# A third block of tokens on its own condition, and a small second block whose low parts lie beside its high parts

## The chip, the cores and the metric

The kernel runs on one core of one Trainium2 chip. The metric is the device time of one execution in microseconds (us); the median of several runs is compared with that of the changed kernel.

## The reference

Chunked attention feeds a dense layer pair with a gated activation, and that feeds a mixture of eight experts. Only the expert part is touched:

```python
expert_idx = np.argmax(x @ w_gate, axis=1)      # one expert for each of 1536 tokens
for i in range(N):                              # the first `capacity` = 384 tokens of each expert
    ...
h = np.maximum(np.einsum('ecd,edf->ecf', disp, w1), 0.0)   # 512 -> 1024
y = np.einsum('ecf,efd->ecd', h, w2)                       # 1024 -> 512
out[i] = gate_w[i] * y[expert_idx[i], pos[i]]
```

Worked out from the reference with its inputs, the experts get, in the order in which the kernel takes them (`EORDER`), 224, 291, 128, 160, 128, 256, 160 and 189 tokens. They are called e0 to e7 here, by place in that order.

## The kernel before, in words

Every product of two 32-bit numbers is made of three TensorE matmuls: each operand is held as a rounded high part and a low part (the remainder), and high x high, high x low and low x high are added up in PSUM. An expert's tokens come in blocks of 128, gathered by GpSimd (`load`, L808), transposed by TensorE (`trans`, L825) and split by ScalarE and VectorE (L829, L830).

The code for one expert from e1 on is two arms of a branch on the token count, read from a register by each engine (L1260). Up to 128 tokens, the arm `one` runs the first block alone (`block`: 64 matmuls with its transposes). Above, the arm `more` runs two blocks together: `layer1` (96 matmuls of 256 columns, L858; its high parts by ScalarE, L861, its low parts by VectorE, L862), the transposes of the next expert's two blocks (`next_trans`), `layer2` of block 0 (24 matmuls of 512 columns, L925: 8 pieces of 128 rows, three products each), and then `rest`. In `rest` a second branch (L963) asks for more than 256 tokens: if so, it transposes block 2, runs `layer2` of block 1 and the whole `block` 2; if not, only `layer2` of block 1. Whichever block comes last leaves its result in the PSUM tile `ylast`, and `after_arms` scales it (ScalarE, L945) and sends it to its rows of `out` (GpSimd, L946). The other blocks are scaled and sent where they end. The order of the sends is fixed: each writes `out`, so each waits until the one before has landed.

e0 has a code of its own (`after_first`), with the branches L992 and L1000, whose bodies are skipped with these inputs. In a `with tc.If` without an else, an engine that skips the body first waits until its own earlier work is done.

Inside each arm ScalarE and VectorE also split the weights for this expert's second layer and the next expert's first one (L289 and L294, eight pieces of 128x1024 each in `more`). A scheduler decides the order of the instructions on each engine within a stretch without branches, by the order of the code and priorities; the branch itself is one such piece, which it may put ahead of work written earlier.

```python
hi, lo = t[:, 0, :, o:o + P], t[:, 1, :, o:o + P]   # a split tile: [part, piece, token]
for n, (hz, wz) in enumerate(((0, 0), (0, 1), (1, 0))):
    nc.tensor.matmul(ps, lhsT=h[:, hz, fc, o:o + P], rhs=w[:, wz, fc % 4, :], ...)
```

Of the kernel before, what the change touches and what calls it, by code (L numbers as in the profile page):

```python
# [9 lines left out]
F32 = mybir.dt.float32  # L10
# [6 lines left out]
ALU = mybir.AluOpType  # L17
# [4 lines left out]
P = 128  # L22
# [65 lines left out]
def kernel(  # L88
# [14 lines left out]
    nc = tc.nc  # L103
# [19 lines left out]
    F2 = F // P  # L123
    NCB = max(2, -(-cap // P))
# [128 lines left out]
    class Piece(SimpleNamespace):  # L253
# [19 lines left out]
        def rest(self, act=True):  # L273

            low = self.words()[0].bitcast(U32)
            self.r = w_pools["work"].tile([P, KC, P], I32, tag="rest", name="rest")
            if act:
                nc.scalar.activation(out=self.r, in_=low, func=AF.Copy, scale=2.0 ** -29)
            else:
                nc.vector.tensor_scalar(out=self.r, in0=low, scalar1=2.0 ** -29, scalar2=None, op0=ALU.mult)  # L280
# [90 lines left out]
    def w_tile(name, i):  # L371
        while (name, i) not in ready:
            assert flight or wide or w_can_load(), name
            w_pump()
        return where[name].rearrange("p z (c f) -> p z c f", f=512)
# [424 lines left out]
    def expert_parts(e, ep, tp, cnt):  # L800

        ex = EORDER[e]
# [19 lines left out]
        def trans(b):  # L822
            ps = psum("t", "pst")
            for c in range(KC):
                nc.tensor.transpose(ps[:, c * P:(c + 1) * P], xr[b][:, c * P:(c + 1) * P], ident)  # L825
            t, o = xs_of(b)
            hi, lo = t[:, 0, :, o:o + P], t[:, 1, :, o:o + P]
            pv = ps.rearrange("p (c n) -> p c n", n=P)
            act = nc.scalar.activation(out=hi, in_=pv, func=AF.Copy)  # L829
            dve = nc.vector.tensor_tensor(out=lo, in0=pv, in1=hi.bitcast(F32), op=ALU.subtract)  # L830
            return act.ins, dve.ins

        def gate(b):
            sm = tp.tile([P, 1], F32, tag="gs", name="gs")
            nc.scalar.activation(out=tp.tile([P, E], F32, tag="ex", name="ex"), in_=xr[b][:, DM:DM + E], func=AF.Exp, accum_out=sm)  # L835
            g = tp.tile([P, 1], F32, tag="gt", name="gt", bufs=8)
            nc.vector.tensor_scalar(out=sm, in0=sm, scalar1=EPS, scalar2=None, op0=ALU.add)
            nc.vector.reciprocal(out=g, in_=sm)
            gt[b] = g
# [88 lines left out]
        def layer2(b, last):  # L928
            ps = y_of(last)
            layer2_part(b, ps, range(F2))  # L930
            evacuate(b, ps, last)

        ylast = []

        def evacuate(b, ps, last):
# [19 lines left out]
        def after_arms():  # L955
            send(*ylast)

        def rest(b):

            if b == NCB:  # L960
                layer2(b - 1, True)
                return
            with tc.If(cnt[ex] > b * P) as more:  # L963
                trans(b)
                layer2(b - 1, False)
                gate(b)
                later(b)
            with more.Else():
                layer2(b - 1, True)

        def later(b):
            block(b, True)

        def next_trans():
            if e + 1 < E:
# [30 lines left out]
        def more():  # L1006

            for b in range(2, NCB):
                load(b)
            for fc in range(F2):  # L1010
                mm, act = layer1(fc)
                if fc == GFC:
                    after_act = act
                if fc == TFC:
                    after_mm = mm
                if fc in PUMPS:
                    w_next(e)
            with tc.issue_after(after_act):
                for b in range(2):
                    gate(b)  # L1020
            with tc.issue_after(after_mm):
                next_trans()
            layer2(0, False)
            with tc.high_priority(offset=-LOWER2):
                while w_next(e):
                    pass
            rest(2)
        return SimpleNamespace(load=load, trans=trans, xs_of=xs_of, one=one, more=more, after_first=after_first,
                               before_arms=before_arms, after_arms=after_arms)


    with ExitStack() as st:
# [34 lines left out]
        def after_attention(_):  # L1067
# [21 lines left out]
            n=lambda g: step_n(g, nc.vector), N=lambda g: step_n(g, nc.gpsimd), d=step_d, p=step_p, e=step_e,  # L1089
# [130 lines left out]
    with ExitStack() as st:  # L1220
        wp3 = ctx.enter_context(tc.tile_pool(name="wp3", bufs=1, side="left"))
        ep = st.enter_context(tc.tile_pool(name="ep", bufs=1, side="right"))
        tp = st.enter_context(tc.tile_pool(name="tp", bufs=2, side="right"))
        pst = st.enter_context(tc.tile_pool(name="ps_t", bufs=2, space=PSUM))
        ps2 = st.enter_context(tc.tile_pool(name="ps_h2", bufs=4, space=PSUM))
        ps3 = st.enter_context(tc.tile_pool(name="ps_y", bufs=1, space=PSUM))
        ps_pools["t"] = (pst, "t", [P, 512])
        ps_pools["h"] = (ps2, "h", [P, 512])
        ps_pools["y"] = (ps3, "y", [P, 512])
        ps_pools["yl"] = (ps3, "yl", [P, 512])  # L1230
        free_slots.append(wp3.tile([P, 2, 2048], F32R, name="w5"))
        late_raw(RAWS)
        parts = [expert_parts(e, ep, tp, cnt) for e in range(E)]
        not_before.append(parts[0].load(1))
        with ExitStack() as behind:
            for i in parts[0].trans(1):
                behind.enter_context(tc.issue_after(i))
            w_loads(8)
            while w_next(-1):
                pass  # L1240
        w_end[0] = len(pieces)
        with tc.high_priority(offset=LOADS):
            w_loads(8 * (F // 512))
        not_before.clear()
        for e in range(E):
            if e + 1 < E:
                for b in range(2):
                    parts[e + 1].load(b)
                parts[e + 1].xs_of(0)
            if e == 0:  # L1250
                with tc.high_priority(offset=LOADS):
                    w_loads(8 * (F // 512))
                first_block.send()
                parts[0].after_first()
            else:
                parts[e].before_arms()
                with tc.high_priority(offset=LOADS):
                    w_loads(8 * (F // 512))
                before = w_state()
                with tc.If(cnt[EORDER[e]] > P) as full:  # L1260
                    parts[e].more()
                after = w_state()
                w_back(before)
                with full.Else():
                    parts[e].one()
                assert w_state() == after
                parts[e].after_arms()
            for j in range(F // 512):
                w_free(("w1", e, j))
            for j in range(F // 512):  # L1270
                w_free(("w2", e, j))
# [70 lines left out]
```

## Time and profile before

| | us |
|---|---|
| median of three runs | 543.0 (542.32 to 543.14) |
| the profiled execution | 540.01 |
| its span, first to last instruction | 538.2 |
| TensorE (PE) busy | 516.9, 96% of the span |
| VectorE (DVE) busy | 311.0, 58% |
| ScalarE (ACT) busy | 272.6, 51% |
| GpSimd (POOL) busy | 85.1, 16% |

The profiled execution took 3.0 us less than the median of the runs. PE is the instruction stream of the matmuls, PEld the loading of their stationary operand, which runs beside them. In a row of the timeline, the bracket says how long the engine sat idle before it and what ended that; "issue" is time in which it waited for nothing that the profile shows, and a trailing q (PEq) is the engine's sequencer. An engine's clock (PEclk) is the granted share of its full speed.

### The profile page before, as it was taken

The page shows a single profiled execution, that of the slowest core. Times are in us where ns is not written, and L with a number is a line of the kernel's source. Part 1 is how long each engine was busy: PE and PEld are TensorE (multiplying, and loading weights), DVE is VectorE, ACT ScalarE, POOL GpSimd, SP SyncE. Part 2 cuts the span into 40 slices and gives each one's busy share as a digit, 9 for nine tenths or more (in the row PEclk, how much of TensorE's full clock was granted, in tenths as well). Part 3 has the DMA queues.
Part 4 walks back from the last instruction along what each step waited for, and adds up shares of the span by engine and source line. Part 5 has one row for each costly group of instructions (what it writes and reads, how often), then busy time and mean ns, then how long its engine had stood idle before and what let it go on. Part 6 is the DMA issues. An engine that isn't in the chain of part 4 may idle for free. (4 is left out here: it accounts for less than half of the span.)

```text
span 538.2 us, 10665 instructions
## 1 busy us (share of the span) xinstructions
PE 516.9 (96%) x4211; PEld 445.0 (83%) x4211; DVE 311.0 (58%) x627; ACT 272.6 (51%) x551; POOL 85.1 (16%) x92
## 2 busy tenths in 40 slices
PE   8898999999999999999999999999988997999995
PEld 4686888899988999889988887779777976989893
DVE  4899799995229722228375446457314944947250
ACT  2786879773237422235254334457235925938231
POOL 3211012222001100004100000232022222201111
PEclk9999999999999999999999999999998998999999
DMA  8985654342003530000168213597524884885000
GB/s 287 328 315 193 238 174 141 120 158 79 1 0 119 184 130 1 1 0 2 37 210 264 80 41 98 161 319 260 181 62 160 269 324 146 279 328 196 23 26 31
DMA packets 38955, 80.29 MB, mean 149 GB/s; under 512 B 4009, under 2 KB 10153, under 8 KB 38890
## 3 DMA queue, kind: packets, MB, share of 16 engines
q1 hardware_dynamic: 36010, 70.66, 38.3%
q0 software_dynamic: 2880, 8.74, 5.1%
q8 instruction: 43, 0.70, 0.5%
q14 instruction: 22, 0.18, 0.1%
HBM read 69.90 MB, written 10.27 MB: 149 GB/s over the span
## 5 line engine op out<-in xcount | busy, mean ns | idle before, releaser
L584 PE MATMUL acc<-w,g 128*128 128x512 f32 x576 | 153.3, 400 | 1.1 <-DVE w L294 0.7
L541 PEld LDWEIGHTS psh<-xT,w 128*128 128x128 f32 x1152 | 146.7, 188 | 7.4
L541 PE MATMUL psh<-xT,w 128*128 128x256 f32 x1152 | 151.1, 280 | 0.0
L584 PEld LDWEIGHTS acc<-w,g 128*128 128x128 f32 x576 | 100.6, 188 | 21.5 <-issue 2.1
L556 ACT ACTIVATE sg<-psh 128x256 f32<-128x256 f32 x96 | 36.8, 384 | 128.2 <-PE psh L541 127.8
L294 DVE TENSOR_TENSOR w<-raw,w 128x1024 fp32r<-128x1024 f32 x64 | 77.2, 1220 | 41.5 <-ACT w L289 38.0
L564 DVE TENSOR_TENSOR g<-sg,g 128x256 fp32r<-128x256 f32 x87 | 40.3, 463 | 77.8 <-ACT g L560 74.7
L925 PE MATMUL psy<-w,hT 128*128 128x512 f32 x336 | 82.7, 400 | 0.3 <-ACT y L945 0.3
L925 PEld LDWEIGHTS psy<-w,hT 128*128 128x128 f32 x336 | 62.0, 188 | 15.3 <-ACT y L945 0.6
L289 ACT ACTIVATE w<-raw 128x1024 fp32r<-128x1024 f32 x64 | 66.3, 1060 | 2.8 <-PE acc L584 2.2
L858 PEld LDWEIGHTS psh<-xs,w 128*128 128x128 f32 x480 | 58.0, 188 | 1.1 <-issue 0.7
L858 PE MATMUL psh<-xs,w 128*128 128x256 f32 x480 | 58.3, 282 | 0.3 <-PEq L1000 0.3
L560 ACT ACTIVATE g<-psh 128x256 fp32r<-128x256 f32 x96 | 36.2, 380 | 0.0
L595 DVE SCALAR_TENSOR_TENSOR x<-acc,x 128x512 f32<-128x512 f32 x36 | 24.3, 687 | 18.2 <-PE acc L584 18.0
L880 PE MATMUL psh<-w,xs 128*128 128x512 f32 x96 | 27.4, 438 | 7.0 <-ACT w L289 2.9
L880 PEld LDWEIGHTS psh<-w,xs 128*128 128x128 f32 x96 | 19.6, 210 | 12.7 <-issue 7.2
L808 POOL DMA_INDIRECT xr<-rows,taker x20 | 24.2, 1211 | 23.6 <-DVE w L294 16.9
L294 DVE TENSOR_TENSOR w<-w,w 128x512 fp32r<-128x512 f32 x27 | 21.6, 802 | 9.5 <-ACT w L289 9.3
L270 DVE SCALAR_TENSOR_TENSOR w<-raw,w 128x512 int32<-128x512 int32 x32 | 23.4, 734 | 0.1
L259 ACT ACTIVATE w<-raw 128x512 f32<-128x512 f32 x32 | 21.1, 670 | 1.4 <-DMA raw<-in_w_out_dram 1.2
L289 ACT ACTIVATE w<-w 128x512 fp32r<-128x512 f32 x32 | 20.0, 628 | 3.5 <-POOL w L284 2.0
L284 POOL TENSOR_TENSOR w<-w,rest 128x512 int32<-128x512 int32 x8 | 12.1, 1507 | 60.8 <-DVE w L270 55.0
(134 smaller groups left out, 487.2 us busy)
## 6 DMA issues: line engine op xcount, KB each, us to landing
raw<-in_w_dram SPq DMA_DIRECT2D x64, 512.0 KB, 5.0
raw<-in_w_in_dram SPq DMA_DIRECT2D x16, 512.0 KB, 3.8
raw<-in_w_out_dram SPq DMA_DIRECT2D x16, 512.0 KB, 3.3
vt<-in_v_dram SPq DMA_DIRECT2D x12, 512.0 KB, 3.6
kt<-in_k_dram SPq DMA_DIRECT2D x12, 368.0 KB, 6.7
qt<-in_q_dram SPq DMA_DIRECT2D x12, 256.0 KB, 4.1
out_dram<-blank SPq DMA_DIRECT2D x12, 256.0 KB, 4.2
rows<-x SPq DMA_DIRECT2D x5, 520.0 KB, 4.1
```

The source lines that it names most:

```text
L289: nc.scalar.activation(out=w_dst(self.name, self.i, 0), in_=w, func=AF.Copy)
L294: eng.tensor_tensor(out=lo, in0=w, in1=hi.bitcast(F32), op=ALU.subtract)
L541: nc.tensor.matmul(ps, lhsT=w[:, wz, c, i * P:(i + 1) * P], rhs=xT[tb][:, xz, c, :], start=n == 0, stop=n == 3 * KC - 1)
L556: nc.scalar.activation(out=sg_t[u], in_=h_t[u], func=AF.Silu, scale=1.702)
L560: g_last[:1] = [nc.scalar.activation(out=g[:, 0], in_=h_t.pop(u), func=AF.Silu, scale=1.702).ins]
L564: lo = eng.tensor_tensor(out=g[:, 1], in0=sg_t.pop(u), in1=g[:, 0].bitcast(F32), op=ALU.subtract)
L584: nc.tensor.matmul(acc_t[tb][s], lhsT=g[:, gz, s * P:(s + 1) * P], rhs=w[:, wz, wi, :], start=i == 0 and n == 0, stop=u == last_of(k, tb) ...
L595: nc.vector.scalar_tensor_tensor(out=dst, in0=acc_t[tb][s], scalar=1 / 1.702, in1=dst, op0=ALU.mult, op1=ALU.add)
L808: return nc.gpsimd.indirect_dma_start(out=t, out_offset=None, in_=rows[:, :], in_offset=bass.IndirectOffsetOnAxis(ap=taker[:, b, ex:ex + 1 ...
L858: mm = nc.tensor.matmul(ps, lhsT=w[:, wz, c, f0:f0 + P], rhs=t[:, xz, c, :], start=m == 0, stop=m == 3 * KC - 1)
L880: nc.tensor.matmul(p1[j], lhsT=x[:, xz, c, o:o + P], rhs=w[:, wz, c, :], start=(xz, wz, c) == (0, 0, 0), stop=(xz, wz, c) == (1, 0, KC - 1))
L925: nc.tensor.matmul(ps, lhsT=h[:, hz, fc, o:o + P], rhs=w[:, wz, fc % 4, :], start=fc == 0 and n == 0, stop=fc == F2 - 1 and n == 2)
```

## The change

Two things. `rest` is taken out of the arm `more` and becomes a condition of its own, behind `after_arms`, for every expert from e1 on (so also behind the arm `one`): above 256 tokens it transposes block 2 and runs it, with its own send. And in `more`, where the second block has at most 64 tokens (an expert of at most 192: here e3, e6 and e7), a new `layer2_few` runs the second layer of that block. VectorE copies the low parts of its 64 tokens into the columns beside the 64 high parts, so that one matmul of the pair multiplies both with the high part of the weights (rows 0 to 63 and 64 to 127 of the result), and a second one of 64 columns adds high x low. At the end VectorE adds the lower half of the result to the upper one. Otherwise `layer2` of block 1 runs as before, into `ylast`.

```diff
+        def layer2_few(b):
+            n = P // 2
+            h = hT_of(b)
+            o = b * P
+            nc.vector.tensor_copy(h[:, 0, :, o + n:o + P], h[:, 1, :, o:o + n])
+            ps = y_of(True)
+            for fc in range(F2):
+                w = w_tile(("w2", e, fc // 4), (fc % 4) // 2)
+                both = [(ps, h[:, 0, fc, o:o + P], w[:, 0, fc % 4, :]), (ps[:n], h[:, 0, fc, o:o + n], w[:, 1, fc % 4, :])]
+                for i, (out_, x, y) in enumerate(both if fc < F2 - 1 else both[::-1]):
+                    nc.tensor.matmul(out_, lhsT=x, rhs=y, start=fc == 0 and i == 0, stop=fc == F2 - 1 and i == 1)
+            t = ep.tile([P, 512], F32, tag="hs", name="few", bufs=2)
+            nc.vector.tensor_copy(t[:n], ps[n:])
+            nc.vector.tensor_tensor(out=ps[:n], in0=ps[:n], in1=t[:n], op=ALU.add)
+            evacuate(b, ps, True)
...
-        def rest(b):
-            if b == NCB:
-                layer2(b - 1, True)
-                return
-            with tc.If(cnt[ex] > b * P) as more:
-                trans(b)
-                layer2(b - 1, False)
-                gate(b)
-                later(b)
-            with more.Else():
-                layer2(b - 1, True)
+        def rest():
+            for b in range(2, NCB):
+                with tc.If(cnt[ex] > b * P):
+                    trans(b)
+                    gate(b)
+                    block(b, False)
...
             layer2(0, False)
             with tc.high_priority(offset=-LOWER2):
                 while w_next(e):
                     pass
-            rest(2)
+            with tc.If(cnt[ex] < P + P // 2 + 1) as small:
+                layer2_few(1)
+            with small.Else():
+                layer2(1, True)
...
                 parts[e].after_arms()
+                parts[e].rest()
```

On TensorE, the arm `more` of e6 stood like this, from the transposes of the next expert's blocks on (psy is the result of a `layer2`, L963 the branch in `rest`):

```order
L825 MATMUL pst<-ident,xr 128x128 x8
L925 MATMUL psy<-w_94,hT 128x512 x12
L925 MATMUL psy<-w_93,hT 128x512 x12
L963 COMPARE_AND_BRANCH
L825 MATMUL pst<-ident,xr 128x128 x4
...
L963 UNCONDITIONAL_BRANCH
L925 MATMUL psy<-w_94,hT 128x512 x12
L925 MATMUL psy<-w_93,hT 128x512 x12
L963 UNCONDITIONAL_BRANCH
```

It now stands like this (L1036 is the branch on 192 tokens, L944 the matmuls of `layer2_few`):

```order
L825 MATMUL pst<-ident,xr 128x128 x8
L925 MATMUL psy<-w_94,hT 128x512 x5
L1036 COMPARE_AND_BRANCH
L944 MATMUL psy<-w_94,hT 128x512
L944 MATMUL psy<-w_94,hT 64x512
...
L1036 UNCONDITIONAL_BRANCH
L925 MATMUL psy<-w_94,hT 128x512 x12
L925 MATMUL psy<-w_93,hT 128x512 x12
L1036 UNCONDITIONAL_BRANCH
L925 MATMUL psy<-w_94,hT 128x512 x7
L925 MATMUL psy<-w_93,hT 128x512 x12
```

The branch with the second block has moved into the second layer of block 0: five of its 24 matmuls stand ahead, 19 behind.

On VectorE, the end of the same arm of e6 was this (L294 splits a weight piece, L862 writes a low part of the first layer, L830 that of the next expert's tokens):

```order
L294 TENSOR_TENSOR w_4506<-raw_3_3362,w_4506 128x1024 [waits DMAHW6_49]
L862 SCALAR_TENSOR_TENSOR hT<-psh,hT 128x256 [waits Activation_49]
L830 TENSOR_TENSOR xs<-pst,xs 128x4x128 [waits Activation_49] x2
L963 COMPARE_AND_BRANCH
```

And now it is this:

```order
L862 SCALAR_TENSOR_TENSOR hT<-psh,hT 128x256 [waits Activation_49]
L830 TENSOR_TENSOR xs<-pst,xs 128x4x128 [waits Activation_49]
L1036 COMPARE_AND_BRANCH
L938 COPY hT<-hT 128x8x64 [waits DVE_49]
L946 COPY few<-psy 64x512 [waits PE_49]
L947 TENSOR_TENSOR psy<-psy,few 64x512 [waits DVE_49]
L1036 UNCONDITIONAL_BRANCH
L1036 UNCONDITIONAL_BRANCH [waits DVE_49]
L830 TENSOR_TENSOR xs<-pst,xs 128x4x128 [waits Activation_49]
```

The copy of the low parts stands behind all the weight pieces, the last low part of the first layer and one of the two L830.

On GpSimd, the end of the program (e7) was this, with the send of block 0 (y, taker) ahead of the branch and that of `ylast` (y, tl) behind the arms:

```order
L946 DMA out_dram<-y,taker 1536x512 [waits DMASW5_49,Activation_49]
L963 COMPARE_AND_BRANCH
...
L946 DMA out_dram<-y,tl 1536x512 [waits DMASW5_49,DMASW7_49,DMASW0_49,Activation_49]
```

And now it is this:

```order
L1036 UNCONDITIONAL_BRANCH
L963 DMA out_dram<-y,taker 1536x512 [waits DMASW5_49,DMASW4_49,Activation_49]
L1272 UNCONDITIONAL_BRANCH
...
L963 DMA out_dram<-y,tl 1536x512 [waits DMASW5_49,DMASW7_49,DMASW4_49,Activation_49]
L978 COMPARE_AND_BRANCH
```

The send of block 0 has moved behind the second block's branch, next to the last send, which waits for it (DMASW7).

## Rows read from the trace of the kernel before

**Rows 1.** The page: its head and part 1 (busy time of each engine).

```profile
span 538.2 us, 10665 instructions
PE 516.9 (96%) x4211; PEld 445.0 (83%) x4211; DVE 311.0 (58%) x627; ACT 272.6 (51%) x551; POOL 85.1 (16%) x92
```

**Rows 2.** Groups of TensorE by line: busy us, mean ns, idle before.

```profile
L925 PE MATMUL psy<-w,hT 128*128 128x512 f32 x336 | 82.7, 400 | 0.3 <-ACT y L945 0.3
L858 PE MATMUL psh<-xs,w 128*128 128x256 f32 x480 | 58.3, 282 | 0.3 <-PEq L1000 0.3
```

**Rows 3.** Timeline of TensorE, e6 and e7: start, length, what.

```profile
496.64 1.03 PE L825 MATMUL pst<-ident,xr 128*128 128x128 f32 x8
497.43 11.48 PE L925 MATMUL psy<-w,hT 128*128 128x512 f32 x48
508.75 11.59 PE L858 MATMUL psh<-xs,w 128*128 128x256 f32 x96
520.18 11.40 PE L925 MATMUL psy<-w,hT 128*128 128x512 f32 x48
```

**Rows 4.** Timeline of TensorE, the third block of e1 and the start of e2.

```profile
383.34 0.60 PE L825 MATMUL pst<-ident,xr 128*128 128x128 f32 x4
384.28 5.88 PE L925 MATMUL psy<-w,hT 128*128 128x512 f32 x24 [0.34 <-ACT y L945]
390.00 4.36 PE L880 MATMUL psh<-w,xs 128*128 128x512 f32 x18
405.14 5.99 PE L880 MATMUL psh<-w,xs 128*128 128x512 f32 x18 [2.91 <-ACT w L289]
```

**Rows 5.** Timeline of TensorE, e3's second layer and the start of e4.

```profile
432.13 11.49 PE L925 MATMUL psy<-w,hT 128*128 128x512 f32 x48
444.63 0.47 PE L880 MATMUL psh<-w,xs 128*128 128x512 f32 x1 [1.01 <-ACT y L945]
447.38 5.47 PE L880 MATMUL psh<-w,xs 128*128 128x512 f32 x17 [2.28 <-issue]
```

**Rows 6.** Windows after those two waits: length, busy times by engine, granted clock, DMA.

```profile
407.00:409.00 2.00, 2.00 (x6) 1.52 (x6) 0.00 (x0) 0.00 (x0) 1.00 (x1) 0.50 0.90 282
447.30:449.00 1.70, 1.62 (x4) 1.28 (x4) 0.00 (x0) 0.00 (x0) 1.39 (x2) 0.50 0.59 178
```

**Rows 7.** Timeline of TensorE behind the skipped branches L992 and L1000 of e0.

```profile
351.63 4.48 PE L880 MATMUL psh<-w,xs 128*128 128x512 f32 x18 [0.83 <-ACT xs L829]
365.32 11.69 PE L858 MATMUL psh<-xs,w 128*128 128x256 f32 x96 [0.32 <-PEq L1000]
```

**Rows 8.** Timeline of VectorE at the end of the first layer: e3, e6, e7.

```profile
434.99 1.28 DVE L830 TENSOR_TENSOR xs<-pst,xs 128x512 fp32r<-128x512 f32 x2
499.34 1.28 DVE L830 TENSOR_TENSOR xs<-pst,xs 128x512 fp32r<-128x512 f32 x2
520.80 0.42 DVE L862 SCALAR_TENSOR_TENSOR hT<-psh,hT 128x256 fp32r<-128x256 f32 x1 [0.99 <-ACT hT L861]
```

**Rows 9.** Groups of VectorE by line and shape: one source, and two.

```profile
L263 DVE TENSOR_SCALAR w<-w 128x512 f32<-128x512 f32 x32 | 14.8, 471 | 7.2 <-ACT w L259 7.2
L830 DVE TENSOR_TENSOR xs<-pst,xs 128x512 fp32r<-128x512 f32 x16 | 10.4, 685 | 5.2 <-ACT xs L829 5.0
```

**Rows 10.** Timeline of ScalarE at e1's third block: send's scaling, gate, token split.

```profile
383.54 0.69 ACT L945 ACTIVATE y<-psy,gt 128x512 f32<-128x512 f32 x1 [4.97 <-PE psy L925]
384.12 0.20 ACT L835 ACTIVATE ex<-xr 128x8 f32<-128x8 f32 x1
384.31 0.59 ACT L829 ACTIVATE xs<-pst 128x512 fp32r<-128x512 f32 x1
```

**Rows 11.** The end: GpSimd's last two sends, and the first one's flight in the chain.

```profile
526.98 1.00 POOL L946 DMA_INDIRECT out_dram<-y,taker  x1 [14.09 <-ACTq L963]
532.71 1.00 POOL L946 DMA_INDIRECT out_dram<-y,tl  x1 [4.42 <-ACT y L945]
526.98 2.76 DMA out_dram<-y,taker
```

More of the change, by code (lines that the diff above doesn't have):

```diff
@@ L956, in after_arms @@
             send(*ylast)
-        def rest(b):
-            if b == NCB:
-                layer2(b - 1, True)
-                return
-            with tc.If(cnt[ex] > b * P) as more:
-                trans(b)
-                layer2(b - 1, False)
-                gate(b)
-                later(b)
-            with more.Else():
-                layer2(b - 1, True)
-        def later(b):
-            block(b, True)
+        def rest():
[4 more added lines that the diff above has]
+                    block(b, False)
         def next_trans():
@@ L1026, in more @@
                     pass
-            rest(2)
-        return SimpleNamespace(load=load, trans=trans, xs_of=xs_of, one=one, more=more, after_first=after_first,
+            with tc.If(cnt[ex] < P + P // 2 + 1) as small:
+                layer2_few(1)
+            with small.Else():
+                layer2(1, True)
+        return SimpleNamespace(load=load, trans=trans, xs_of=xs_of, one=one, more=more, rest=rest, after_first=after_first,
                                before_arms=before_arms, after_arms=after_arms)
```

## The prediction

> **What bounds the kernel now.** I read the page first: TensorE is busy for 516.9 of 538.2 us [rows 1], so time is won or lost where its stream gets shorter or has holes. Then the groups by line, to see which arms ran: 480 matmuls at L858 are five passes through `more` of 96 each [rows 2], as the token counts say (e1, e3, e5, e6, e7); of these e3, e6 and e7 have at most 192 tokens. Then TensorE's timeline through the experts. From e6 to e7 there is no hole at all: 11.48 us of second layers end where the next first layer starts [rows 3]. So a matmul taken out there is worth its full time, and a wait put in costs its full time. The holes stand elsewhere: at e1's third block [rows 4] and where the arm `one` starts, at e2 (2.91 us) and e4 (1.01 and, after a single matmul, 2.28 us, "issue") [rows 4, 5]. Last, VectorE and ScalarE where the first layer ends, since the new copy queues there, and the chain at the end of the program.
>
> All terms go against the profiled execution, 540.0 us; the median of the runs is 543.0, and I add the sum to that.
>
> **The matmuls saved.** `layer2_few` has 16 in place of 24. A matmul of 512 columns comes every 11.40 / 48 = 0.238 us [rows 3], and one of 256 columns every 11.59 / 96 = 0.121 us: the moving columns set the pace, not the width of the result. So the 64-wide ones cost 0.238 us too, and eight less are worth 1.9 us, three times: **-5.7 us**. If the 64-wide ones were quicker, at most some tenths more.
>
> **The copy ahead of them.** The first L944 waits for the copy of the low parts. Before, the second block's matmuls came after 24 others; now only five stand ahead, because the branch has moved into block 0's second layer. Nothing behind a waiting matmul can pass it, so the 19 others, which need nothing new, wait too. When would TensorE be there, and when is the copy done?
> - e3: TensorE at 432.13 + 5 x 0.239 = 433.3 [rows 5]. VectorE is late with its weight pieces: its L830 pair starts at 434.99 and one of the two takes 0.64 [rows 8], so it ends at 435.6. The copy moves 512 numbers per partition from SBUF to SBUF; the trace has none, the nearest is a one-source instruction of that size, 0.47 us, the dearer bound a two-source one that reads PSUM, 0.69 [rows 9]. I take 0.47, and 0.1 each for VectorE's branch and for the wake-up (an estimate; the skipped branch of rows 7 cost TensorE 0.32 for both). Done at 436.3: **3.0 us** of waiting.
> - e6: TensorE at 497.43 + 1.19 = 498.6 [rows 3], the copy done at 499.34 + 0.64 + 0.67 = 500.65 [rows 8]: 2.0 us. Ahead of e6, ScalarE now has the sends of both blocks of e5 to scale, one more at 0.58 us from start to start [rows 10], before it can start on the weights that VectorE waits for; TensorE is itself 0.3 later (below). So 2.3 us.
> - e7: no next expert, so no L830 and few weight pieces. TensorE at 520.18 + 1.19 = 521.4, the last low part done at 520.80 + 0.42 [rows 3, 8], the copy at 521.9: 0.5 us.
>
> Together **+5.8 us** (5.3 to 6.8 with the bounds for the copy and the branch). What follows the matmuls, VectorE's second copy and the addition, some 1.2 us by rows 9, lies beside the 19 matmuls of 4.5 us and costs nothing. So `layer2_few` by itself saves nothing.
>
> **The clock after a hole.** [...] After the hole of 0.83 us the pace was not hurt (18 in 4.48) [rows 7]. The new holes of 3.0 and 2.3 us lie between, close to the larger; I count one fall, **+1.5 us** (0 to 3.0).
>
> **The branch of its own.** Where there are no more than 256 tokens, each engine waits for its own work and jumps over the body. The trace has this: L1000 cost TensorE 0.32 us before e1 [rows 7]. It now stands ahead of e3, e5, e6 and e7 with nothing else to wait for: 4 x 0.32 = **+1.3 us**; ahead of e4 it lies in the hole that is there, behind e7 beside the last sends.
>
> **The third block of e1.** Before, its tokens were transposed ahead of block 1's second layer, and the 24 matmuls covered the split: transposes and wait took 384.28 - 383.34 = 0.94 us [rows 4]. Now nothing covers it. From the last matmul, ScalarE starts after 0.2 us, scales two sends (0.58 each), does the gate (0.19) and splits (0.59) [rows 10], with 0.1 for its branch 2.3 us until the block can start: **+1.4 us**. Bounds: 0.3, if the split came ahead of the sends as in rows 7 (0.83 of waiting plus transposes), and 2.0.
>
> **The end.** Before, e7's block 0 was sent beside the last matmuls. Now its send starts when they end, and the last one waits until it has landed. The first send took 2.76 us from its issue [rows 11], and the second can't start before: **+2.8 us**; the scaling of the second hides in that.
>
> **The start of e2.** There TensorE jumps from the end of e1 over an arm and a whole `more`. Counting matmuls jumped over with nothing executed in between: 324 ahead of e2 (24 + 64 + 236), 300 ahead of e4, both with a hole that the profile puts to nothing but "issue" at TensorE's weight load; 64 ahead of e6 and e7, and there no hole [rows 3 to 5]. Now `more` has 168, and ahead of e2 the body of the third block is executed: 168 are left. That is nearer to 64 than to 300, so I take the hole to shrink to the one that a wait for the send leaves, 1.01 us as at e4: -1.9, and the slow clock behind it goes, -1.63: **-3.5 us** (0 to -4.5). Ahead of e4 there are 292, and I leave it as it is; ahead of e6 and e7 124, and I count nothing.
>
> **Sum:** -5.7 + 5.8 + 1.5 + 1.3 + 1.4 + 2.8 - 3.5 = +3.6 us, 543.6 by the profiled execution, **546.6 us** as a median.
>
> **The rivals.**
> - *The hole at e2 stays.* For it: 168 matmuls are still more than twice what was jumped over freely. Then +3.5: 550.1 us. Chance 0.25. [...]
> - *More holes.* Both new waits bring the clock down, or one of the jumps of 124 matmuls shows: +1.5 to +3.3, around 549.5 us. Chance 0.14.
> - *The hole at e4 closes too*, because the jump over it is now made in three steps, with a stop of the sequencer at the skipped branch: -2.28 - 1.35, 543.0 us, no change. Against it: the distance is the same. Chance 0.11.
> - *The copy is in time* (the other side). If VectorE were through with its pieces when TensorE gets there, 5.8 and 1.5 us go: 539.3 us, faster. It decides where the two waits of e3 and e6 together stay under 1.5 us and the clock holds. For it: the lag is not VectorE's nature, at e7, with half the weight pieces, it is nearly gone [rows 8]; a slower TensorE elsewhere could let it catch up. Against it: at e3 and e6 the copy stands behind all eight pieces on VectorE, and the changes at the borders delay ScalarE, which feeds them. Chance 0.08.
>
> **Numbers.** The forecast has a chance of 0.42 (545 to 548.3 on its own). The range from 543.0 to 551.0 us leaves out the fourth rival and the upper tail. A measurement of this kernel can tell about 0.2%, 1.1 us, from no change: faster 0.09, same 0.12, slower 0.79.
>
> **What would show it.** In the changed kernel's timeline: 16 L944 in about 3.8 us, three times; TensorE's wait ahead of the first, put to VectorE's L938, near 3.0, 2.3 and 0.5 us; granted clock 0.5 behind one of them; 0.3 us ahead of e3, e5, e6 and e7, put to PEq; some 2.3 us from e1's second layers to its third block, ended by ScalarE's L829; e2's first matmul about 1 us after e1's last, without a slow stretch; and the last send issued some 3.9 us after the last matmul (1.1 before), behind the landing of the other. The forecast is wrong if L944 starts without a wait, if e2 keeps its hole, or if the holes bring the clock down more often than once.

## The result and the profile after

The changed kernel takes 549.2 us (median of 6 runs, 547.0 to 550.1), the kernel before beside it 542.7 us: a ratio of 1.0125, with a 95% interval from 1.009 to 1.016. That is +6.5 us, where +3.6 had been forecast; 549.2 lies inside the range of 543 to 551. The profiled execution took 550.0 us with a span of 548.2. Some 3.2 us of the 10.0 us between the two spans lie ahead of the changed code (the transposes ahead of e0's last block stand at 353.37 in place of 350.21), where runs of one kernel differ, too (353.37 and 350.63 in two executions of the change); behind that point the change costs 6.8 us, which fits the medians. Two executions in the sets of the experiments below took 1014 and 1020 us, nearly twice as long as all the others, and are left out of every median and ratio.

First the page's head and its part 1, against [rows 1]:

```profile
span 548.2 us, 10729 instructions
PE 514.4 (94%) x4183; PEld 440.9 (80%) x4187; DVE 319.0 (58%) x636; ACT 273.8 (50%) x551; POOL 87.4 (16%) x92
```

Then groups of TensorE by line, against [rows 2]:

```profile
L925 PE MATMUL psy<-w,hT 128*128 128x512 f32 x264 | 66.0, 400 | 0.0
L858 PE MATMUL psh<-xs,w 128*128 128x256 f32 x480 | 62.2, 292 | 5.1 <-DVEq L978 3.4 <-PEq L978 1.3 <-PEq L1009 0.4
L944 PE MATMUL psy<-w,hT 128*128 128x512 f32 (+1 forms) x48 | 11.8, 399 | 2.4 <-DVE hT L938 2.4
```

72 matmuls of L925 have become 48 of L944, as said. But TensorE is busy for 94% in place of 96%: the holes grew. New is what stands behind L858: ahead of its 480 matmuls TensorE is idle for 5.1 us, of which the skips make 1.7.

Then the timeline of the changed kernel, TensorE first, with two rows of VectorE and the last rows of ScalarE and GpSimd. L962 is the scaling of a result (L945 before), L963 the send (L946), L978 the condition in `rest`.

```profile
392.15 0.60 PE L825 MATMUL pst<-ident,xr 128*128 128x128 f32 x4
394.34 4.47 PE L880 MATMUL psh<-w,xs 128*128 128x512 f32 x18 [1.59 <-ACT xs L829]
...
406.51 4.38 PE L880 MATMUL psh<-w,xs 128*128 128x512 f32 x18
...
417.43 1.28 DVE L830 TENSOR_TENSOR xs<-pst,xs 128x512 fp32r<-128x512 f32 x2
418.63 3.48 DVE L294 TENSOR_TENSOR w<-raw,w 128x1024 fp32r<-128x1024 f32 x3
...
420.06 0.38 PE L858 MATMUL psh<-xs,w 128*128 128x256 f32 x1 [0.32 <-PEq L978]
422.17 13.15 PE L858 MATMUL psh<-xs,w 128*128 128x256 f32 x95 [1.73 <-DVEq L978]
...
437.04 0.42 DVE L938 CAST hT<-hT 128x512 fp32r<-128x512 f32 x1
...
437.60 3.95 PE L944 MATMUL psy<-w,hT 128*128 128x512 f32 x16 [0.23 <-DVE hT L938]
...
449.89 5.97 PE L880 MATMUL psh<-w,xs 128*128 128x512 f32 x18 [3.89 <-ACT w L289]
...
467.15 13.15 PE L858 MATMUL psh<-xs,w 128*128 128x256 f32 x95 [1.72 <-DVEq L978]
...
508.42 3.94 PE L944 MATMUL psy<-w,hT 128*128 128x512 f32 x16 [1.88 <-DVE hT L938]
...
530.30 3.95 PE L944 MATMUL psy<-w,hT 128*128 128x512 f32 x16 [0.33 <-DVE hT L938]
534.09 4.61 PE L925 MATMUL psy<-w,hT 128*128 128x512 f32 x19
...
538.74 0.69 ACT L962 ACTIVATE y<-psy,gt 128x512 f32<-128x512 f32 x1 [9.50 <-PE psy L925]
...
539.71 1.01 POOL L963 DMA_INDIRECT out_dram<-y,taker  x1 [13.60 <-ACT y L962]
543.26 0.98 POOL L963 DMA_INDIRECT out_dram<-y,tl  x1 [2.55 <-DMA out_dram<-y,taker]
```

Read it from the top. e1's third block waits for its split (1.59 us; before it was covered [rows 4]). e2 starts without any hole (before: 2.91 us and a slow stretch [rows 4]). Then comes what nobody had forecast: e3 runs one matmul, stands for 1.73 us and goes on slowly, 95 matmuls in 13.15 us where before 96 took 11.68. The same happens at e5. VectorE's rows show why the time is what it is: the low parts of e3's tokens (L830) are done at 418.7, but TensorE goes on at 422.17, when VectorE has also finished the three weight pieces behind them (418.63 + 3.48 = 422.11). The waits for the copy (L938) are 0.23, 1.88 and 0.33 us. At the end, the two last sends stand 3.55 us apart, the second behind the landing of the first.

The windows of two of these stretches show the clock (the number behind POOL's count), against [rows 6]:

```profile
420.00:421.00 1.00, 0.38 (x1) 0.19 (x1) 1.00 (x2) 0.47 (x1) 0.00 (x0) 1.00 0.84 305
...
423.00:425.00 2.00, 2.00 (x11) 2.00 (x11) 1.75 (x2) 1.36 (x3) 1.68 (x2) 0.50 0.80 163
```

Behind the hole of 1.73 us the granted clock is 0.50, where it was 1.00 ahead of it.

The same stretches of the two profiled executions, from one expert's first matmul to the next one's:

| stretch | before, us | after, us | difference |
|---|---|---|---|
| e1 to its third block | 24.68 | 25.83 | +1.15 |
| third block to e2 | 15.14 | 12.17 | -2.97 |
| e2 | 14.68 | 13.55 | -1.13 |
| e3 | 24.81 | 29.83 | +5.02 |
| e4 | 16.93 | 15.17 | -1.76 |
| e5 | 23.56 | 27.66 | +4.10 |
| e6 | 23.63 | 24.41 | +0.78 |
| e7 to the last matmul | 22.83 | 21.57 | -1.26 |
| behind it | 6.62 | 9.50 | +2.88 |

e4's hole is counted with e3 up to its first matmul; before, most of it lay behind that one [rows 5]. The two together cost 3.3 us before and 3.9 after.

### The profile page after: what moved, and what is told of

It reads as the page before. It is cut to its first block, busy times and chain, and to the rows that moved or that the text cites. A ratio compares the mean times of both kernels' runs of the same rounds, so it can differ in the third digit from the quotient of the medians.

```text
span 548.2 us, 10729 instructions
## 1 busy us (share of the span) xinstructions
PE 514.4 (94%) x4183; PEld 440.9 (80%) x4187; DVE 319.0 (58%) x636; ACT 273.8 (50%) x551; POOL 87.4 (16%) x92
## 4 chain that ended last, share of the span: by engine, by line
PE 52%; issue 24%; DMA 13%; POOL 4%; DVE 3%; ACT 3%; SPq 1%; another core or an unknown queue 0%; POOLq 0%; ACTq 0%
PE acc L584 23%; PE psh L541 22%; DMA xr<-rows,taker 8%; POOL xr L808 2%; PE pse L499 2%; DMA out_dram<-y,taker 2%; DMA raw<-in_w_out_dram 1%; PE pss L429 1%; DMA raw<-in_w_in_dram 1%; PE psr L609 1%; DMA raw<-in_w_dram 1%; PE lg L622 1%; PE psd L482 1%; PE psh L880 1%; POOL w L284 1%
## 5 line engine op out<-in xcount | busy, mean ns | idle before, releaser
L294 DVE TENSOR_TENSOR w<-raw,w 128x1024 fp32r<-128x1024 f32 x64 | 77.2, 1219 | 37.0 <-ACT w L289 36.9
L858 PE MATMUL psh<-xs,w 128*128 128x256 f32 x480 | 62.2, 292 | 5.1 <-DVEq L978 3.4
L858 PEld LDWEIGHTS psh<-xs,w 128*128 128x128 f32 x480 | 60.8, 198 | 7.6 <-DVEq L978 3.8
L925 PE MATMUL psy<-w,hT 128*128 128x512 f32 x264 | 66.0, 400 | 0.0
L925 PEld LDWEIGHTS psy<-w,hT 128*128 128x128 f32 x264 | 48.5, 188 | 11.5 <-DVE hT L894 0.9
L962 ACT ACTIVATE y<-psy,gt 128x512 f32<-128x512 f32 x7 | 4.8, 688 | 56.4 <-PE psy L925 56.4
L880 PE MATMUL psh<-w,xs 128*128 128x512 f32 x96 | 25.9, 422 | 6.3 <-ACT w L289 3.9
L294 DVE TENSOR_TENSOR w<-w,w 128x512 fp32r<-128x512 f32 x27 | 21.4, 795 | 7.9 <-ACT w L289 7.6
```

What stands on the lines that cost most here:

```text
L294: eng.tensor_tensor(out=lo, in0=w, in1=hi.bitcast(F32), op=ALU.subtract)
L858: mm = nc.tensor.matmul(ps, lhsT=w[:, wz, c, f0:f0 + P], rhs=t[:, xz, c, :], start=m == 0, stop=m == 3 * KC - 1)
L880: nc.tensor.matmul(p1[j], lhsT=x[:, xz, c, o:o + P], rhs=w[:, wz, c, :], start=(xz, wz, c) == (0, 0, 0), stop=(xz, wz, c) == (1, 0, KC - 1))
```

## The experiments

All were run beside the kernel before (541.6 to 542.5 us in these sets). Ratios are given with their 95% intervals. "Few's branch" is the branch on 192 tokens that holds `layer2_few`.

| kernel | median, us | ratio to before |
|---|---|---|
| layer2_few alone | 537.2 | 0.9925 (0.990 to 0.995) |
| branch behind the arms alone | 541.1 | 0.999 (0.997 to 1.001) |
| change, test behind e1 alone | 541.7 | 1.000 (0.998 to 1.003) |
| before, arms swapped | 552.7 | 1.020 (1.017 to 1.023) |
| change, few's branch behind block 0 | 540.9 | 0.997 (0.995 to 1.000) |
| layer2_few alone, no addition | 533.1 | 0.982 (0.979 to 0.986) |
| branch alone, longer body | 545.0 | 1.006 (1.004 to 1.009) |
| few's branch behind block 0, shared code | 535.9 | 0.989 (0.986 to 0.992) |
| layer2_few alone, own send | 541.0 | 0.999 (0.997 to 1.001) |
| branch alone, three copies behind | 534.9 | 0.987 (0.984 to 0.990) |

**Each half alone.** The first kernel keeps `rest` in the arm and puts `layer2_few` into its last else:

```diff
             with more.Else():
-                layer2(b - 1, True)
+                with tc.If(cnt[ex] < P + P // 2 + 1) as small:
+                    layer2_few(b - 1)
+                with small.Else():
+                    layer2(b - 1, True)
```

> The kernel before, with layer2_few alone: the third block stays inside the arm, and layer2_few stands where the last layer2 of block 1 was, behind all 24 matmuls of block 0's second layer. Theory A (the loss of the whole change lies in the branch behind the arms; the copy is in time wherever 24 matmuls stand ahead of it): no wait ahead of the 16 matmuls of e3, e6 and e7, 24 matmuls fewer at 0.238 us, so 542.7 - 5.7 = 537.0 us, 535.5 to 539. Theory B (the prediction's account: the copy is late because VectorE lags, whatever stands ahead): waits of 3.0, 2.3 and 0.5 us and one slow stretch take back all of it, so about 543 to 544 us.

537.2 us. There is no wait ahead of the 16 matmuls, so the copy hides behind 24 others, as theory A says. But the sum came out by other terms than the expectation's. Scaling behind `one` waits for VectorE, and a wait inside e3's and e5's first layer follows; the end is 1.0 us longer; and the half of e4's hole behind its first matmul was absent (the stretch of e4 is 3.8 us shorter). Its timeline:

```profile
423.15 0.69 ACT L962 ACTIVATE y<-psy,gl 128x512 f32<-128x512 f32 x1 [1.90 <-DVE w L294]
...
427.57 6.22 PE L858 MATMUL psh<-xs,w 128*128 128x256 f32 x48 [1.29 <-DVE hT L862]
...
440.12 3.88 PE L944 MATMUL psy<-w,hT 128*128 128x512 f32 x16
445.01 4.44 PE L880 MATMUL psh<-w,xs 128*128 128x512 f32 x18 [1.01 <-issue]
```

The second takes `layer2_few` out of the change:

```diff
-            with tc.If(cnt[ex] < P + P // 2 + 1) as small:
-                layer2_few(1)
-            with small.Else():
-                layer2(1, True)
+            layer2(1, True)
```

> The changed kernel without layer2_few: block 1's second layer always takes 24 matmuls; the third block stands behind the arms as in the change. Theory A (the branch behind the arms costs most: 1.7 us of hole and 1.5 us of slow clock behind each arm `one`, 0.3 at each skip, 2.9 at the end, 1.2 at e1's third block, less 4.1 at e2): 549.2 + 5.7 of matmuls - 2.4 of copy waits = 552.5 us, 550.5 to 554, with the hole ahead of the second matmul of e3 and of e5 as in the changed kernel. Theory B (the prediction's terms for the branch: +1.3 + 1.4 + 2.8 - 3.5): 542.7 + 2.0 = 544.7 us.

541.1 us: both theories were too high, and the branch behind the arms costs nothing in sum. `layer2_few`, worth -4.9 us alone, costs 7 to 8 us beside it. So the loss is in how the two meet.

```profile
417.61 0.36 PE L858 MATMUL psh<-xs,w 128*128 128x256 f32 x1 [0.43 <-DVE w L294]
419.61 11.66 PE L858 MATMUL psh<-xs,w 128*128 128x256 f32 x95 [1.65 <-DVEq L978]
...
444.17 4.43 PE L880 MATMUL psh<-w,xs 128*128 128x512 f32 x18 [0.78 <-PEq L978]
...
459.90 13.06 PE L858 MATMUL psh<-xs,w 128*128 128x256 f32 x95 [1.63 <-DVEq L978]
```

The hole ahead of the second matmul is there without `layer2_few`, at e3 with no slow stretch behind it (95 matmuls in 11.66 us) and at e5 with one (13.06 us). e4 has no hole but the 0.8 us of the skip, and the time behind the last matmul is 6.06 us in place of 9.50: the long end belongs to `layer2_few`'s place, not to the branch.

**Is it the skip?**

```diff
-                parts[e].rest()
+                if e == 1:
+                    parts[e].rest()
```

> The changed kernel with the test for a third block behind e1 alone; it leaves out the third block of the other experts, which these token counts do not have. Theory A (a skipped branch makes each engine finish its own work, and behind an arm `one` VectorE still has three weight pieces, for which TensorE's second matmul of e3 and e5 then waits): the 0.3 us ahead of e3, e5, e6 and e7 and the holes of 1.7 us at e3 and e5 go, with the slow stretches behind them, in all 1.3 + 3.5 + 3.0 = -7.8 us; but VectorE then does not catch up, and the copy ahead of e3's 16 matmuls is waited for again, 2.5 to 3 us in place of 0.2, perhaps with a slow clock behind it (1.5): 543.5 to 546 us. Theory B (the holes at e3 and e5 come from the way into e3's and e5's code, not from the skip): they stay, only the 0.3 us go: about 548 us.

541.7 us, and neither theory as written. Nothing is skipped ahead of e3, and the hole is there:

```profile
417.89 0.38 PE L858 MATMUL psh<-xs,w 128*128 128x256 f32 x1
420.48 13.15 PE L858 MATMUL psh<-xs,w 128*128 128x256 f32 x95 [2.21 <-DVE w L294]
...
435.91 3.95 PE L944 MATMUL psy<-w,hT 128*128 128x512 f32 x16 [0.23 <-DVE hT L938]
...
444.15 4.37 PE L880 MATMUL psh<-w,xs 128*128 128x512 f32 x18
```

At e5 the hole is 2.21 us, too, with no slow stretch behind it (11.66 us). So the skip doesn't make it. e4's hole went too, which pays for most of the 7.5 us; the next experiments take up both.

**What sets the holes at e2 and e4.** In the kernel before, the arms were swapped:

```diff
-                with tc.If(cnt[EORDER[e]] > P) as full:
-                    parts[e].more()
+                with tc.If(cnt[EORDER[e]] < P + 1) as full:
+                    parts[e].one()
```

> The kernel before with its two arms written in the other order (`one` first). Theory A (the holes at e2 and e4 come from the length of the jump over code): TensorE then falls from e1's `more` into e2's `one` with no matmuls jumped over, so the holes of 2.9 us at e2 and of 2.3 us at e4 and the slow stretches behind them go, and the jump of about 300 matmuls now lies ahead of e3 and e5, where holes of 2 to 3 us appear: about 542.7 us in all, 540 to 545. Theory B (they come from what the arm `one` waits for, the send or the weights): they stay at e2 and e4, none appear at e3 and e5, 542.7 us. The place tells the two apart, not the sum.

552.7 us. The places are theory A's, the sizes aren't:

```profile
403.48 4.38 PE L880 MATMUL psh<-w,xs 128*128 128x512 f32 x18
...
423.18 13.13 PE L858 MATMUL psh<-xs,w 128*128 128x256 f32 x96 [6.46 <-issue]
...
448.26 4.36 PE L880 MATMUL psh<-w,xs 128*128 128x512 f32 x18
...
469.05 13.96 PE L858 MATMUL psh<-xs,w 128*128 128x256 f32 x96 [7.57 <-issue]
```

The holes followed the long jump from e2 and e4 to e3 and e5. Why they are 6.5 and 7.6 us there and not 3 stays open.

Then the jump ahead of e4 was made longer in the kernel with the branch alone, by code that is never executed:

```diff
                     block(b, False)
+                    if b == NCB - 1:
+                        with tc.If(cnt[ex] > 8 * P):
+                            layer2_part(b, y_of(False), range(F2))
+                            layer2_part(b, y_of(False), range(F2))
```

> The kernel with the branch behind the arms alone (541.1 us), with 48 more matmuls written at the end of the third block's body, under a condition that never holds, so that nothing more is executed; they lengthen the jump ahead of e4 from 272 to 320 matmuls, and that ahead of e2 (144, behind an executed body) stays nearly as it is. Theory A (a jump over 288 matmuls or more costs a hole, one over 272 or fewer none): a hole of 2.5 to 4 us at e4, which that kernel did not have, perhaps with a slow stretch of 1.5 us behind it, none at e2; 541.1 + 4 = 545 us, 543.5 to 547. Theory B (the hole at e4 comes with layer2_few, by what it makes ScalarE and VectorE wait for): no hole, 541 to 541.7 us with the test that e1 skips.

545.0 us, theory A's time; in the profiled execution (542.9, the shortest of its runs) the hole is smaller than expected, 1.54 us behind five matmuls, with no slow stretch. From e1's third block on, this execution took 3.1 us more than that of the branch alone: 1.8 of them lie between the first matmuls of e4 and e5, where the hole is, and 1.1 ahead of e2, where 0.93 us of waiting have come with the new test, which e1 skips. What makes the other runs of this kernel longer than the profiled one isn't shown. (The expectations count a jump without some of the transposes; by the prediction's count their 272, 288, 312 and 320 are 276, 292, 316 and 324.)

```profile
404.06 4.44 PE L880 MATMUL psh<-w,xs 128*128 128x512 f32 x18 [0.93 <-ACT y L962]
...
444.34 1.40 PE L880 MATMUL psh<-w,xs 128*128 128x512 f32 x5 [0.78 <-PEq L978]
447.28 3.29 PE L880 MATMUL psh<-w,xs 128*128 128x512 f32 x13 [1.54 <-issue]
```

**Few's branch behind block 0.** The change with one thing moved:

```diff
-            layer2(0, False)
             with tc.high_priority(offset=-LOWER2):
                 while w_next(e):
                     pass
-            with tc.If(cnt[ex] < P + P // 2 + 1) as small:
-                layer2_few(1)
-            with small.Else():
-                layer2(1, True)
+            with in_order():
+                layer2(0, False)
+                with tc.If(cnt[ex] < P + P // 2 + 1) as small:
+                    layer2_few(1)
+                with small.Else():
+                    layer2(1, True)
```

> The changed kernel with one thing moved: the branch of layer2_few stands behind all 24 matmuls of block 0's second layer, and on VectorE behind both L830 of the next expert. Theory A (the loss of the whole change comes from that branch standing after 5 of the 24): no wait ahead of the 16 matmuls of e3, e6 and e7 (2.4 us less), block 0 of e7 is sent beside the last matmuls again (end 2 us shorter), and e4 starts without the hole of 3.9 us; what stays is the wait ahead of the second matmul of e3 and e5 (1.65 us), which the kernel with the branch behind the arms alone has too: 541.1 - 5.7 + 1 for the longer end = 536.5 us, 535 to 539. Theory B (the branch behind the arms and layer2_few harm each other wherever the latter stands): 546 to 549 us.

540.9 us, 8.3 less than the change, and outside the ranges of both theories. The copy is in time, the end is 7.63 us in place of 9.50, and the wait ahead of the second matmul has become one of 0.8 us further on. The hole at e4 stayed, though (its jump is now 316), with a slower stretch behind it, and that is what is missing to the 536.5:

```profile
424.22 6.24 PE L858 MATMUL psh<-xs,w 128*128 128x256 f32 x48 [0.83 <-DVE hT L862]
...
436.78 3.89 PE L944 MATMUL psy<-w,hT 128*128 128x512 f32 x16
444.94 6.72 PE L880 MATMUL psh<-w,xs 128*128 128x512 f32 x18 [4.26 <-ACT w L289]
```

The same with shorter code: the 16 matmuls that both cases need stand once, 8 stand under a condition.

```diff
+            both = [(0, wz, fc) for fc in range(F2) for wz in range(2)]
+            products(both[:1])
+            with tc.If(cnt[ex] > P + n):
+                products([(1, 0, fc) for fc in range(F2)])
+            products(both[1:])
```

> The kernel with layer2_few's branch behind block 0 (540.9 us), written shorter: the 16 matmuls that both cases need stand once, and the 8 of the low parts stand under a condition of their own (more than 192 tokens). The jump ahead of e4 falls from 312 to 272 matmuls. Theory A (length): the hole of 4.3 us at e4 goes, and 0.8 stay for the skip; two more conditions in each pass, three of them skipped at 0.3 us, cost about 1.5 us: 540.9 - 3.5 - 1.5 of slow clock + 1.5 = 537.5 us, 536 to 539. Theory B (layer2_few's waits make the hole): it stays, and with the conditions 542 us.

535.9 us, at the lower end of theory A. The hole of 4.26 us is gone, and the 0.83 us of the skip are left. The 18 matmuls behind it take 4.79 us where the branch alone had 4.43:

```profile
442.44 4.79 PE L880 MATMUL psh<-w,xs 128*128 128x512 f32 x18 [0.83 <-PEq L987]
```

Over all kernels: ahead of e4, jumps of 232 and 276 matmuls had no hole beyond 0.8 us of skip, jumps of 292 to 340 had 1.0 to 4.3 us. The size doesn't follow the length: 340 left 1.01 us with `layer2_few` alone and 2.49 us without its addition, 292 left 3.89 us in the change. What TensorE waits for in such a hole no run shows.

**The scaling that waits for VectorE.** The expected cause was that one arm lets VectorE write `ylast`. This kernel leaves the product of the low parts out of the result:

```diff
-            t = ep.tile([P, 512], F32, tag="hs", name="few", bufs=2)
-            nc.vector.tensor_copy(t[:n], ps[n:])
-            nc.vector.tensor_tensor(out=ps[:n], in0=ps[:n], in1=t[:n], op=ALU.add)
```

> The kernel with layer2_few alone (537.2 us), without VectorE's copy and addition at its end; it leaves out the addition of the product of the low parts, so that VectorE no longer writes the tile that after_arms scales. Theory A (because one arm lets VectorE write that tile, ScalarE's scaling behind every arm waits for VectorE, which behind `one` has three weight pieces left: 1.9 us, and the low parts of e3's and e5's first layer come 1.3 us late): ScalarE's wait goes, the holes of 1.29 and 1.28 us inside the first layers of e3 and e5 go, and the end is 1 us shorter, in all 537.2 - 3.5 = 533.7 us, 532.5 to 535. Theory B (VectorE is simply late there, with or without that wait): the holes stay, only the end is 1 us shorter, 536.2 us.

533.1 us, theory A. ScalarE scales without a wait and the first layer has no hole:

```profile
420.51 11.68 PE L858 MATMUL psh<-xs,w 128*128 128x256 f32 x96
...
421.29 0.69 ACT L959 ACTIVATE y<-psy,gl 128x512 f32<-128x512 f32 x1
...
444.90 4.44 PE L880 MATMUL psh<-w,xs 128*128 128x512 f32 x18 [2.49 <-ACT w L289]
```

So VectorE's copy and addition, which lie beside TensorE in every expert but the last, cost 4.1 us: 1.5 behind the last matmul (7.62 against 6.13), and 2.6 by the two holes that follow from the scaling's waits behind `one` (1.90 and 1.89 us). That the sum comes out so well is in part chance: the slow stretch at e2 went (1.5 us less) and the hole at e4 grew from 1.01 to 2.49 us. A whole version without that wait was a miss:

```diff
-            ps = y_of(True)
+            ps = y_of(False)
...
-            evacuate(b, ps, True)
+            nc.tensor.matmul(ylast[0], lhsT=h[:, 0, 0, o:o + P], rhs=w[:, 0, 0, :], start=True, stop=True)
+            evacuate(b, ps, False)
+            nc.gpsimd.tensor_copy(ylast[1], gt[b])
+            nc.gpsimd.memset(ylast[2], NT)
```

> The kernel with layer2_few alone (537.2 us), changed so that VectorE does not write the tile that after_arms scales: layer2_few takes a tile of its own and sends from inside the arm; after_arms then scales a tile filled by one dummy matmul and sends it to rows beyond the output, where it is dropped. The last expert keeps the old second layer. Theory A: ScalarE's wait of 1.9 us behind `one` goes, with the holes of 1.3 us in the first layers of e3 and e5 and what they drag (1.6 and 1.7 us); e7 loses the 1.9 us of its matmuls and gets back 0.4 of its hole and 1.0 at the end; dummies 0.5: 537.2 - 3.3 + 1.0 = 534.9 us, 533.5 to 536.5. Theory B (one more scaling and one more send at the borders, each send waiting for the one before, cost as much): 537 us or more.

541.0 us, theory B: the holes in the first layers did go (e3's and e5's 96 matmuls run in one piece), but new ones came where the arm hands over, since TensorE now waits for a scaling there, and 0.87 us stand ahead of the 16 matmuls of e3 and e6:

```profile
445.89 5.98 PE L880 MATMUL psh<-w,xs 128*128 128x512 f32 x18 [2.29 <-ACT y L965]
...
509.58 11.70 PE L858 MATMUL psh<-xs,w 128*128 128x256 f32 x96 [2.20 <-ACT y L965]
```

**The wait ahead of the second matmul.** In the kernels with the hole (the change, the branch alone, the test behind e1 alone, the longer body; 1.57 to 2.21 us) the last VectorE instruction of `more` is an L830 that TensorE needs next. In those without it (before, the ones with few's branch behind block 0), at least three stand behind it, and `one` has three weight pieces behind its L830. So:

```diff
             with tc.issue_after(after_mm):
-                next_trans()
+                with in_order(only=(mybir.EngineType.DVE,)):
+                    next_trans()
+                    for i in range(3):
+                        nc.vector.tensor_copy(tp.tile([P, 1], F32, tag="gs", name="behind"), gt[0])
```

> The kernel with the branch behind the arms alone (541.1 us), with three copies of one column added on VectorE at the end of the arm `more`, behind both L830 of the next expert; nobody reads them. Theory A (a matmul behind the arms that needs what either arm made waits, in both, until as many VectorE instructions are left as stand behind it in the arm with fewer; `one` has three weight pieces behind its L830 pair, `more` of that kernel has nothing behind its own, so behind `one` TensorE waits for the three pieces): with three behind the pair in `more` too, the holes of 1.65 us ahead of the second matmul of e3 and e5 go, perhaps in part taken by a later wait of up to 0.9 us, and the slow stretch behind the one at e5: 541.1 - 3.3 - 1.5 = 536.3 us, up to 538.5. Theory B (the skipped branch makes VectorE finish its queue and TensorE wait for it): the holes stay, 541.1 us.

534.9 us, below theory A's 536.3. Three useless copies save 6.2 us:

```profile
416.04 11.76 PE L858 MATMUL psh<-xs,w 128*128 128x256 f32 x96 [0.32 <-PEq L978]
...
440.70 4.43 PE L880 MATMUL psh<-w,xs 128*128 128x512 f32 x18 [0.78 <-PEq L978]
```

e3 and e5 start in one piece, at full pace (96 matmuls in 11.76 and 11.77 us). VectorE's instructions from e2 through e3 are the same, in the same order, as with the branch alone, but for the three copies behind the last L830. That the place of L830 in the arm makes the hole is shown by this; that it goes by counting from the end of the arm fits all kernels, but only this one tested it.

**Both kernels once more**, one execution each, to see which holes come again.

> The changed kernel once more, to see which of its holes come again. If they belong to the program: 1.7 us ahead of the second matmul of e3 and e5, 3.9 us at e4, no hole at e2; the slow clock behind the first two may come or not, since holes of 1.6 to 2.2 us have been seen with and without it. 547 to 550 us.

> The kernel before once more, to see which of its holes come again. If they belong to the program: 2.9 us ahead of e2 and 1.0 and 2.3 us at e4, each with a slow stretch behind it. If the hole at e4 is chance (the kernel with layer2_few alone has there 1.0 us only, with code that is no shorter), it may be missing: 541 to 543.5 us.

549.3 and 542.9 us. Every hole came again, with much the same length; the slow stretches didn't all. The kernel before the second time, and then the change:

```profile
450.24 5.51 PE L880 MATMUL psh<-w,xs 128*128 128x512 f32 x17 [2.52 <-issue]
```

```profile
419.40 11.65 PE L858 MATMUL psh<-xs,w 128*128 128x256 f32 x95 [1.72 <-DVEq L978]
...
446.29 7.15 PE L880 MATMUL psh<-w,xs 128*128 128x512 f32 x18 [3.95 <-issue]
...
464.66 13.14 PE L858 MATMUL psh<-xs,w 128*128 128x256 f32 x95 [1.66 <-DVEq L978]
...
505.93 5.51 PE L944 MATMUL psy<-w,hT 128*128 128x512 f32 x16 [1.79 <-DVE hT L938]
```

## Why the prediction was right, and where it was not

The sign, the range and most mechanisms held; the sum was 2.9 us short. 549.2 lies above the 545 to 548.3 that the prediction gave its own account, and near the 549.5 of the rival "More holes", which came in part: the clock fell once more than counted, but behind holes that no term had. That is one of the prediction's own signs of being wrong (the clock brought down more often than once). That the sum isn't further off is luck: the copy's wait was put 3.4 us too high, and 3.45 us of waiting behind the new branch were put at nothing.

- **The matmuls saved** (-5.7): right in kind. In the change, 5, 16 and 19 matmuls take 435.95 to 446.00, 10.05 us with 0.23 of waiting, where 48 took 11.49: 1.7 us for each expert, so -5.0. That the width of the result doesn't set the pace held: the 16, half of them 64 wide, take 3.95 us, 0.247 each, and those of 64 take 393 ns on average, those of 128 404.
- **The copy ahead of them** (+5.8): measured 2.4 (0.23, 1.88, 0.33; the second time 0.84, 1.79 and 0.33). The step that failed is e3's 3.0. VectorE is as late as said, and later: its copy ends at 437.46, not 436.3. But TensorE comes to it 4.1 us later than said, since it stood and crept in the first layer. That is the fourth rival's condition, a slower TensorE elsewhere, at one expert of three. At e6 and e7 (2.3 and 0.5 forecast) the account held, and the 19 others did wait behind the 16: at e7 they start at 534.09, the 16 at 530.30.
- **The clock** (+1.5, 0 to 3.0): the term rests on [rows 4 to 6], where the 18 and 17 matmuls behind the holes at e2 and e4 lost 1.63 and 1.35 us against e1's pace, at a granted clock of 0.50. Measured are two falls of 1.5 us (95 matmuls in 13.15 us, clock 0.50 behind both holes; the second time at e3 in 11.65), at the upper bound, and behind other holes than the copy's. The second time one did stand behind the copy's wait, at e6 (16 matmuls in 5.51 us in place of 3.94).
- **The branch of its own** (+1.3): 0.32 us four times, right. What was not counted is the wait behind it at e3 and e5, 1.73 and 1.72 us: the prediction had the split of the two L830 in its rows of VectorE's order, but used them for the copy's queue alone, not for who needs the one that now stands last.
- **e1's third block** (+1.4): +1.15.
- **The end** (+2.8): +2.88, by the mechanism named, the size partly by luck. The last send is issued 4.56 us after the last matmul (1.13 before, 3.9 forecast), since 0.8 us pass between the first one's landing, 2.76 us after its issue as said, and that issue; but what follows the last send is 0.55 us shorter (4.94 against 5.49). The branch alone doesn't have the long end (6.06 us behind the last matmul), so it comes with few's branch standing inside block 0.
- **The start of e2** (-3.5): -4.4, since no hole at all is left. Its count of matmuls jumped over was a good guide here: 168 went freely, and e4's 292 kept its hole.
- **What `layer2_few` is worth by itself** ("saves nothing"): by the prediction's two terms it saved 2.6 us in the change (-5.0 and +2.4), but its place cost more by other waits, 7 to 8 us beside the branch. Behind 24 matmuls it saves 4.9 us (537.2). VectorE's copy and addition at its end, put at nothing, made no hole in the change; behind 24 matmuls they cost 4.1 us.

Added up by stretches: 5.0 saved and 4.4 at e2, against 7.1 for the two holes at e3 and e5 with what is slow behind them, 2.4 for the copy, 1.3 for the skips, 1.15, 2.88, and 0.6 at e4. That is +6.0; the rest to 6.8 lies in gaps of 0.1 to 0.2 us at the branches.

Two full versions beat both kernels: the change with few's branch behind block 0 and shared code (535.9), and the branch alone with three instructions behind L830 (534.9). Both together were not run.

## What to carry to other kernels

Look where a scheduler puts a branch: standing inside a run of matmuls, it splits the run for all engines, and whatever lands behind it (a result to be sent, the low parts that the next expert needs) is late by the whole arm. Here the end was 9.50 us with the branch inside block 0's matmuls and 7.63 behind them, the whole 549.2 and 540.9. Where two arms met, the next stage waited for the later of two places (1.65 us ahead of the second matmul, gone with three copies at the end of one arm), and an instruction that only one arm has made the scaling behind the other wait, too (1.90 us, gone without VectorE's addition): ask for each engine what stands last in each arm, and which arm writes the tile that is read behind both.

## What the runs showed of the hardware that was not expected

- The clock after a hole is not settled by the hole's length alone. In the fourteen traces of this case, from e0's last block on, 18 matmuls of 512 columns took 4.44 to 4.49 us behind holes of 0.83 to 1.59 us (4.79 behind one of 0.83, in the kernel with shared code). Behind the eight holes of 2.88 us and more, 18 of them took 5.97 to 7.15 us and 96 of 256 columns 13.13 and 13.96 (11.68 without a hole); where the granted clock was read there, it was 0.50 (behind 2.91 us) and 0.52 (3.89). Between, it went both ways, with holes of the same length at the same place (1.73 us with 95 matmuls in 13.15 us behind it, 1.72 us with 11.65; 2.49 and 2.75 us in the kernel without the addition, with 18 matmuls in 4.44 and 4.45 us).
- A jump over code that is never executed cost time: 48 matmuls more in a body that is skipped, under a test of their own, made the kernel some 4 us slower (541.1 to 545.0). In the profiled executions 1.8 us of it lie at the longer jump and 1.1 us at the new test.
